# Normalizing the rests of q and k in place, loading raw weights one step further ahead, and two new orders in a fused attention and SwiGLU kernel

**Chip, cores, metric.** One core of one Trainium2 chip. The metric is the device time of one execution in microseconds (us); the kernel before takes 1638.8 us (median of 4 runs). TensorE is written PE, VectorE DVE, ScalarE ACT, GpSimd POOL and the DMA-issuing SyncE SP, as in the profiles.

## The reference, cut to what matters

```python
# q, k, v: (8, 12, 448, 64); d_model 768, d_ff 1536; the FFN weights come as float64
q_n = q / sqrt(mean(q*q, -1) + 1e-6) * g_q          # k_n likewise with g_k
attn = softmax(q_n @ k_n.T / 8)                     # per batch entry and head
x    = (attn @ v) as (3584, 768)
xn   = x / sqrt(mean(x*x, -1) + 1e-6) * rms_g
g    = xn @ w_gate
out  = (g * sigmoid(g) * (xn @ w_val)) @ w_out
```

## The kernel before

A sequence of 448 rows is three tiles of 128 rows and a *rest* of 64. Heads are worked on in pairs: a *group* `g` is one pair of one sequence, six groups make a sequence. While PE does the attention of sequence b+1, the products of the FFN of sequence b fill its gaps. Four parts matter here.

**The rests.** Rests of q lie on 64 partitions, rests of k on the other 64. q's are normalized in place; k's stay as they are, and their factor `rr` is applied later, as a scale of the exponential:

```python
def norm_rests(b, lo, hi):
    ...                                        # ACT squares, DVE sums them into ms
    def rms():                                 # POOL
        rq = small.tile([D, n, 2], F32, name="rq")
        nc.gpsimd.tensor_scalar(ms, ms, D * 1e-6, None, ALU.add)
        nc.gpsimd.tensor_tensor(rq, ms[0:D], mhalf[0:D, ...], ALU.pow)
        nc.gpsimd.tensor_tensor(rest[0:D], rest[0:D], rq..., ALU.mult)
    def rms_k():                               # POOL, two more pows
        for place in range(2):
            nc.gpsimd.tensor_tensor(st["rr", b][own(place), lo:hi], ms[own(1), :, place], mhalf[own(1), 0:n], ALU.pow)
...
nc.scalar.activation(e, ps[:, 0:S], ACT.Exp, scale=st["rr", b][:, hp:hp + 1])   # ACT, rests' exponential
```

**The conversion of the weights.** 72 pieces of float64 are turned into float32 on the chip, in a pipeline of turns that are strewn between the other work:

```python
raw_pool, cv_pool = pool("c_raw", 6), pool("c_cv", 6)
def convert():                                 # turn n
    ...
    if 0 <= n - 4 < len(pieces): ...           # POOL adds the halves of piece n-4 (frees raw and cv)
    if 0 <= n - 3 < len(pieces): ...           # DVE joins piece n-3
    if 0 <= n - 2 < len(pieces): ...           # ACT splits piece n-2 (needs raw, takes a cv buffer)
    if n < len(pieces): ...                    # SP loads piece n into a raw buffer
    if 0 <= n - 6 < len(pieces): keep(...)     # SP stores the finished piece
    if turn_of["n"] == TURNS:                  # conversion over: cv buffers become weight blocks
        free_w.extend(cv_pool.tile([128, BW], F32, name="top") for _ in range(6))
```

Together with 25 fixed ones this gives 31 weight blocks of 128x384 from then on.

**Derived weights.** The FFN of later sequences uses seven products instead of eight (Strassen). The sums of weights that this needs, T1 to T4, are made once, by DVE, while sequence 1's FFN runs. Each needs a free block, so the number of blocks decides how early a derivation can stand in the program (which is built, in a fixed order, by counting free blocks). Seven such products make a *quad*; sequence 1 begins with its first.

**The order on PE** in the first groups (0 to 6, which the prediction calls the *direct stage*), and just before sequence 0's FFN:

```python
# groups 1 to 6                          # group 7
pe(lambda: score(g, (1,)))               pe(lambda: values(g - 1))
pe(lambda: sums(g - 1))                  pe(lambda: score(g, (1,)))
pe(lambda: score(g, (2,)))               pe(lambda: rms_x(0))
                                         pe(lambda: score(g, (2,)))
                                         pe(lambda: sums(g - 1))
                                         pe(lambda: norm_x(0))
```

Of the kernel before, what the change touches and what calls it, by code (L numbers as in the profile page):

```python
# [8 lines left out]
F32 = mybir.dt.float32  # L9
I32 = mybir.dt.int32  # L10
U32 = mybir.dt.uint32
I64 = mybir.dt.int64
ALU = mybir.AluOpType
ACT = mybir.ActivationFunctionType
# [8 lines left out]
NPAIR = H // 2  # L23
# [312 lines left out]
def safe_scores(  # L336
# [22 lines left out]
    def pool(name, bufs, **kw):  # L359
        return ctx.enter_context(tc.tile_pool(name=name, bufs=bufs, **kw))  # L360
# [3 lines left out]
    qk_pool, v_pool, qn_pool, qkT_pool = pool("c_qk", 4), pool("c_v", 3), pool("c_qn", 1), pool("c_qkT", 2)  # L364
    e_pool, tmp, y_pool, rest_pool = pool("c_e", 11), pool("c_tmp", 1), pool("c_y", 2), pool("c_rest", 2)
    x_pool, s_pool, slots = pool("c_x", 4), pool("c_xs", 3), pool("c_slots", 1)
    raw_pool, cv_pool = pool("c_raw", 6), pool("c_cv", 6)
    scratch = pool("c_dram", 1, space=DRAM)
    ps_s, ps_m, ps_f = pool("c_ps_s", 4, space=PSUM), pool("c_ps_m", 1, space=PSUM), pool("c_ps_f", 3, space=PSUM)

# [8 lines left out]
    def after(n, fn):  # L379
        due.append((now["t"] + n, fn))  # L380
# [14 lines left out]
    def own(j):  # L395
        return slice(j * D, (j + 1) * D)
# [42 lines left out]
    def norm_rests(b, lo, hi):  # L439

        if b >= B:
            return
        n = hi - lo
        rest = st["rest", b][:, lo:hi]
        sq = tmp.tile([128, n, 2, D], F32, name="sq", tag="sq", bufs=2)
        nc.scalar.activation(sq, rest, ACT.Square)
        if lo == 0:
            st["rr", b] = tmp.tile([128, NPAIR], F32, name="rr", tag="rr", bufs=2)
        ms = small.tile([128, n, 2], F32, name="msr")
        after(1, lambda: nc.vector.tensor_reduce(out=ms, in_=sq, axis=AX_X, op=ALU.add))  # L450

        def rms():
            rq = small.tile([D, n, 2], F32, name="rq")
            nc.gpsimd.tensor_scalar(ms, ms, D * 1e-6, None, ALU.add)
            nc.gpsimd.tensor_tensor(rq, ms[0:D], mhalf[0:D, 0:2 * n].rearrange("p (n h) -> p n h", h=2), ALU.pow)
            nc.gpsimd.tensor_tensor(rest[0:D], rest[0:D], rq.unsqueeze(3).to_broadcast([D, n, 2, D]), ALU.mult)

        def rms_k():
            for place in range(2):
                nc.gpsimd.tensor_tensor(st["rr", b][own(place), lo:hi], ms[own(1), :, place], mhalf[own(1), 0:n], ALU.pow)  # L460

        after(1 if b == 0 else 2, rms)
        after(2, rms_k)

    def direct(g):

# [93 lines left out]
    def rests(g):  # L560

        if g < NG:
            ps = ps_s.tile([128, 512], F32, name="sc", tag="s")
            for r in (own(0), own(1)):
                nc.tensor.matmul(ps[r, 0:S], lhsT=st["kT", g][r, LAST], rhs=st["qT", g][r, :], start=True, stop=True)  # L565
        if g:
            b, hp = divmod(g - 1, NPAIR)
            vr, e = st["vr", b][:, hp], st["e", g - 1, "rest"]
            av = st["av", g - 1] = ps_m.tile([128, 512], F32, name="av", tag="m")
            for j in range(2):  # L570
                nc.tensor.matmul(av[own(j), 0:S], lhsT=vr[across(j)], rhs=e[across(j)], start=True, stop=False,
                                 skip_group_check=True)
            if direct(g - 1):
                den = st["den", g - 1] = ps_f.tile([128, 512], F32, name="den", tag="f")
                for j in range(2):
                    nc.tensor.matmul(den[own(j), 0:S], lhsT=ones[across(j)], rhs=e[across(j)], start=True, stop=False,
                                     skip_group_check=True)
        if g < NG:
            b, hp = divmod(g, NPAIR)
            e = st["e", g, "rest"] = e_pool.tile([128, S], F32, name="e")  # L580
            nc.scalar.activation(e, ps[:, 0:S], ACT.Exp, scale=st["rr", b][:, hp:hp + 1])  # L581

    def values(g):

# [115 lines left out]
    def block():  # L700

        if free_w:
            return free_w.pop(0), free_w
        return free_h.pop(0), free_h
# [8 lines left out]
    def data(key):  # L713
        return st[key][0][:, 0:BW]
# [34 lines left out]
            cols = moe_w_out[fc * 128:(fc + 1) * 128, n * HALF:(n + 1) * HALF]  # L749
            pieces.append((("wo", 0, *block_of(n, fc)), cols.rearrange("p (a n) -> p a n", a=1)))  # L750
    turn_of = {"n": 0}
    TURNS = len(pieces) + 6

    def home(key):
        if key[0] == "w":
# [3 lines left out]
    def keep(key):  # L759
        nc.sync.dma_start(out=home(key), in_=data(key))  # L760

    def convert():

        n = turn_of["n"]
        if n >= TURNS or not room(1):
            return False
        turn_of["n"] += 1
        if 0 <= n - 4 < len(pieces):
            key = pieces[n - 4][0]
            st[key] = block()  # L770
            lo, top = st.pop(("cv", n - 4))
            nc.gpsimd.tensor_tensor(data(key).bitcast(I32), top, lo, ALU.add)  # L772
        if 0 <= n - 3 < len(pieces):
            st["cv", n - 3] = join(*st.pop(("cv", n - 3)))
        if 0 <= n - 2 < len(pieces):
            st["cv", n - 2] = split(st.pop(("raw", n - 2)))
        if n < len(pieces):
            st["raw", n] = load_raw(pieces[n][1])
        if 0 <= n - 6 < len(pieces):
            keep(pieces[n - 6][0])  # L780
        if turn_of["n"] == TURNS:

            free_w.extend(cv_pool.tile([128, BW], F32, name="top") for _ in range(6))
        return True


# [345 lines left out]
    def gate_value_items(b):  # L1132

        if b == 0:
            return [(3 * S, 4 * (fc + 1) + 6, 0, fn) for fc in range(NFC) for fn in plain(fc)]
        return [(6 * HT, TURNS, 8 * (fp + 1) if b == 1 else 0, fn) for fp in range(NFP) for fn in quad(b, fp)]

    def out_items(b):
        if b >= FIRST_O:
            return [(NFP // 2 * HALF, TURNS, 0, fn) for fn in out_strassen(b)]  # L1140
        tiles = 3 + b % 2
        return [(NFC // OUT_PARTS * HALF, 4 * NFC + NFC * (n + 1) + 6, 0, lambda a=(b, n, i, part, i == tiles - 1): project_out(*a))
                for n in range(2) for i in range(tiles) for part in range(OUT_PARTS)]


# [108 lines left out]
    for g in range(NG + 1):  # L1254
        b, hp = divmod(g, NPAIR)
        if g:
            load_pair(g + 3)
        if hp == 2:
            for i in range(2):
                load_rests(b + 1, i, nc.sync)  # L1260
            load_v_rests(b + 1)
        if g == 0:
            pe(lambda: score(0, (0,)))
            pe(lambda: rests(0))
            pe(lambda: score(0, (1, 2)))
            squares(2, 0)
            squares(2, 1)
            for i in range(2):
                pe(lambda: turn(1, i))
            for _ in range(3):  # L1270
                convert()
            load_pair(3)
            load_v(2)
            convert()
            load_rows()
            continue
        if g <= NPAIR:
            pe(lambda: score(g, (0,)))
            squares(g + 2, 0)
            squares(g + 2, 1)  # L1280
            convert()
            if g > 1:
                pe(lambda: turn(g + 1, 0))
                some_rests(g)
                pe(lambda: turn(g + 1, 1))
            pe(lambda: rests(g))
            pe(lambda: values(g - 1))
            if g == 1:
                pe(lambda: turn(g + 1, 0))
                some_rests(g)  # L1290
                pe(lambda: turn(g + 1, 1))
            load_v(g + 2)
            convert()
            pe(lambda: score(g, (1,)))
            pe(lambda: sums(g - 1))
            pe(lambda: score(g, (2,)))
            convert()
            if g == 2:
                bound()
            continue  # L1300

        pe(lambda: (rests(g), score(g, (0,)) if g < NG else None))
        pe(lambda: values(g - 1))
        load_v(g + 2)
        if g == NPAIR + 1:
            pe(lambda: score(g, (1,)))
            pe(lambda: rms_x(0))
            pe(lambda: score(g, (2,)))
        pe(lambda: sums(g - 1))
        if g == NPAIR + 1:  # L1310
            pe(lambda: norm_x(0))
            begin(0, 15)
        elif g < NG:
            pe(lambda: score(g, (1, 2)))
        if hp:
            fill()
            squares(g + 2, 0)
            squares(g + 2, 1)
            pe(lambda: turn(g + 1, 0))
            some_rests(g)  # L1320
            fill()
            pe(lambda: turn(g + 1, 1))
            fill()
            continue
        fill(3)
        pe(lambda: turn(g + 1, 0))
        fill(1)
        pe(lambda: rms_x(b - 1))
        squares(g + 2, 0)
        squares(g + 2, 1)  # L1330
        pe(lambda: turn(g + 1, 1))
        fill(len(todo))
        begin(b - 1, 16)
        pe(lambda: norm_x(b - 1))
        fill()
# [41 lines left out]
```

## Time and profile before

| | before |
|---|---|
| time, median of 4 runs (range) | 1638.8 us (1636.4 to 1639.8) |
| PE busy, of a span of 1636.6 us | 1593.6 us |
| POOL / DVE / ACT busy | 678.3 / 857.5 / 475.7 us |
| mean granted clock of PE | 0.990 |

PE is the bound, so the reading is of its idle stretches. A row of an engine's timeline has the start (us), the time that the row covers (us), the engine, the source line, output and inputs, shapes, how many instructions, and in brackets the idle time before it and what ended that. Rows of PE in the first 300 us are shown with the prediction below. Here is how sequence 1's FFN begins (340.23), waits, and ends where its output projection begins (475.50); PE's timeline of the kernel before:

```profile
340.23 2.44 PE L887 MATMUL ff<-x,w 128*128 128x224 f32 x12
...
370.21 3.67 PE L887 MATMUL ff<-x,w 128*128 128x224 f32 x18 [2.02 <-ACT p L920]
...
399.99 1.40 PE L887 MATMUL ff<-xs,top 128*128 128x224 f32 x6 [1.39 <-DVE u L899]
...
467.43 0.55 PE L519 MATMUL tr<-ident,qk 128*128 128x128 f32 x3 [0.31 <-DVE kT L523]
...
475.50 4.69 PE L1085 MATMUL ff<-w,h 128*128 128x384 f32 x14
```

This stretch of 135.27 us, called *stretch 1* below, has 5.66 us of idle PE: the three waits shown and 0.81, 0.23 and 0.90 us on DVE's u.

And POOL's rows for the rests, from its groups of instructions (busy us and mean ns of one stand after the bar; with its smaller forms, rr comes to 34 instructions and 29.8 us):

```profile
L460 POOL TENSOR_TENSOR rr<-msr,mhalf 64x3 f32<-64x3 f32 x30 | 27.3, 911 | 1.8
L455 POOL TENSOR_TENSOR rq<-msr,mhalf 64x6 f32<-64x6 f32 x15 | 21.5, 1436 | 1.3
L456 POOL TENSOR_TENSOR rest<-rest,rq 64x384 f32<-64x384 f32 x15 | 13.6, 908 | 1.2
```

### The profile page before, as it was taken

To read this page: it belongs to the slowest core of one execution; us is meant where nothing else is said; L and a number is where in the kernel's file an instruction comes from. 1 tells how busy PE (TensorE), PEld (TensorE's weight loads), DVE (VectorE), ACT (ScalarE), POOL (GpSimd) and SP (SyncE) were. 2 spreads that over 40 slices of the span, in tenths; PEclk is the share of its full clock that TensorE was granted. 3 is DMA by queue.
4 is the path that set the end of the run, shared out by engine and by line. 5 is a ranking of instruction groups with operands and counts; after the bars stand their busy time and mean duration, and the time that the engine had idled before them with its cause. 6 is when DMAs were issued, how large, how long until landed. Compare 5 with 4: busy or idle time off the path is not lost.

```text
span 1636.6 us, 21588 instructions
## 1 busy us (share of the span) xinstructions
PE 1593.6 (97%) x7328; PEld 1124.5 (69%) x7328; DVE 857.5 (52%) x1490; ACT 475.7 (29%) x944; POOL 678.3 (41%) x706
## 2 busy tenths in 40 slices
PE   7979999998999999999999999999999999999998
PEld 3334445577865787758885588847877587969974
DVE  4879769569872354525564245533655235433431
ACT  5745454322232223222322223222232123100110
POOL 7857777445434442434542245324634322200000
PEclk8999999999999999999999999999999999999999
DMA  7656656557775654485554655556544564557651
GB/s 180 193 158 185 217 163 185 161 178 239 227 227 144 208 160 131 125 257 154 157 151 139 173 162 155 144 185 203 160 135 116 165 178 116 149 182 237 174 143 51
DMA packets 264587, 276.81 MB, mean 169 GB/s; under 512 B 79124, under 2 KB 261396, under 8 KB 264468
## 3 DMA queue, kind: packets, MB, share of 16 engines
q1 hardware_dynamic: 263540, 275.15, 56.4%
q8 instruction: 60, 0.98, 0.3%
q14 instruction: 59, 0.48, 0.1%
q10 hardware_dynamic: 800, 0.20, 0.1%
q0 software_dynamic: 128, 0.00, 0.0%
HBM read 235.93 MB, written 39.32 MB: 168 GB/s over the span
## 4 chain that ended last, share of the span: by engine, by line
PE 85%; DVE 6%; POOL 3%; DMA 2%; issue 1%; SPq 1%; ACT 1%; POOLq 0%; DVEq 0%; ACTq 0%
PE ff L887 38%; PE ff L1085 21%; PE sc L535 6%; PE av L588 6%; PE ff L982 3%; PE ff L1116 3%; PE den L601 2%; PE sc L565 2%; PE tr L519 2%; DVE rd L609 1%; POOL w L772 1%; DVE rd L605 1%; DVE w L844 1%; POOL rs L498 1%; POOL es L552 1%
## 5 line engine op out<-in xcount | busy, mean ns | idle before, releaser
L887 PE MATMUL ff<-x,w 128*128 128x224 f32 x1608 | 326.7, 353 | 3.7 <-ACT p L920 2.0
L887 PEld LDWEIGHTS ff<-x,w 128*128 128x128 f32 x1608 | 301.6, 190 | 12.7 <-issue 5.9
L545 POOL TENSOR_TENSOR es<-e 128x448 f32<-128x448 f32 x82 | 91.3, 1134 | 512.1 <-ACT e L539 512.1
L887 PE MATMUL ff<-xs,w 128*128 128x224 f32 x1248 | 256.3, 353 | 0.3 <-DVE cc L899 0.2
L887 PEld LDWEIGHTS ff<-xs,w 128*128 128x128 f32 x1248 | 234.0, 190 | 5.6 <-issue 4.6
L552 POOL TENSOR_TENSOR es<-es,e 64x448 f32<-64x448 f32 (+1 forms) x164 | 193.2, 1189 | 6.3
L609 DVE RECIPROCAL rd<-rd 128x448 f32<-128x448 f32 x41 | 121.0, 2952 | 142.0 <-ACT rd L608 142.0
L1085 PE MATMUL ff<-w,h 128*128 128x384 f32 x568 | 192.6, 487 | 0.0
L539 ACT ACTIVATE e<-sc,rs 128x448 f32<-128x448 f32 x288 | 162.8, 634 | 52.9 <-PE sc L535 51.3
L1085 PEld LDWEIGHTS ff<-w,h 128*128 128x128 f32 x568 | 106.4, 190 | 74.1 <-issue 3.9
L535 PE MATMUL sc<-qT,kT 64*128 64x448 f32 x576 | 141.2, 589 | 10.1 <-ACT e L581 7.5
L588 PE MATMUL av<-e,vt 128*64 128x448 f32 x576 | 119.4, 550 | 0.0
L535 PEld LDWEIGHTS sc<-qT,kT 64*128 64x128 f32 x576 | 55.5, 190 | 91.5 <-issue 73.7
L1116 PE MATMUL ff<-x,w 128*128 128x448 f32 x288 | 114.4, 551 | 3.3 <-DVE x L655 3.3
L498 POOL TENSOR_TENSOR rs<-ms,mhalf 128x12 f32<-128x12 f32 (+1 forms) x50 | 114.7, 2295 | 4.2
L1085 PE MATMUL ff<-w,so 128*128 128x384 f32 x302 | 104.6, 488 | 2.0 <-DVE y L1046 2.0
L899 DVE TENSOR_TENSOR cc<-ff,u 128x448 f32<-128x448 f32 x84 | 52.3, 623 | 87.3 <-PE ff L887 87.1
L1116 PEld LDWEIGHTS ff<-x,w 128*128 128x128 f32 x288 | 54.5, 194 | 56.2 <-issue 50.6
L772 POOL TENSOR_TENSOR w<-top,raw 128x384 int32<-128x384 int32 x72 | 76.9, 1083 | 35.7 <-DVE top L736 19.6
L588 PEld LDWEIGHTS av<-e,vt 128*64 128x64 f32 x576 | 37.2, 137 | 77.3 <-issue 73.9
L1085 PEld LDWEIGHTS ff<-w,so 128*128 128x128 f32 x302 | 56.5, 190 | 42.3 <-DVE y L1046 3.9
L887 PE MATMUL ff<-x,top 128*128 128x224 f32 x408 | 85.4, 354 | 0.0
(124 smaller groups left out, 1997.0 us busy)
## 6 DMA issues: line engine op xcount, KB each, us to landing
w<-kept SPq DMA_DIRECT2D x443, 192.0 KB, 3.1
w<-kept_o SPq DMA_DIRECT2D x270, 192.0 KB, 2.6
top<-kept SPq DMA_DIRECT2D x109, 192.0 KB, 3.2
kept<-w SPq DMA_DIRECT2D x90, 192.0 KB, 3.8
top<-kept_o SPq DMA_DIRECT2D x66, 192.0 KB, 2.8
qk<-in_q_dram SPq DMA_DIRECT2D x48, 192.0 KB, 3.5
qk<-in_k_dram SPq DMA_DIRECT2D x96, 96.0 KB, 3.3
vt<-in_v_dram SPq DMA_DIRECT2D x48, 192.0 KB, 2.5
```

The source lines that it names most:

```text
L498: nc.gpsimd.tensor_tensor(st["rs", g][:, cols], ms, mhalf[:, cols], ALU.pow)
L535: nc.tensor.matmul(ps[:, 0:S], lhsT=kT[r, c * 128:(c + 1) * 128], rhs=qT[r, :], start=True, stop=True)
L539: nc.scalar.activation(e, ps[:, 0:S], ACT.Exp, scale=rs[:, n:n + 1])
L545: nc.gpsimd.tensor_tensor(es, st["e", g, 0, j], st["e", g, 1, j], ALU.add)
L552: nc.gpsimd.tensor_tensor(es[r], es[r], e[r], ALU.add)
L588: nc.tensor.matmul(av[own(j), 0:S], lhsT=vt[:, j, c], rhs=st["e", g, c, j], start=False, stop=(c == NK - 1), skip_group_check=True)
L609: nc.vector.reciprocal(rd, rd)
L772: nc.gpsimd.tensor_tensor(data(key).bitcast(I32), top, lo, ALU.add)
L887: nc.tensor.matmul(bank[:, w * HT:(w + 1) * HT], lhsT=wt[:, c * 128:(c + 1) * 128], rhs=x[:, c, :], start=onto is None and w == c == 0, st ...
L899: nc.vector.tensor_tensor(add[name], ps[:, 0:S], add[other], ALU.add)
L1085: nc.tensor.matmul(ps, lhsT=a, rhs=data(("wo", b, name, c)), start=first and c == 0, stop=c == NFP - 1, skip_group_check=True)
L1116: nc.tensor.matmul(bank[w][:, 0:S], lhsT=data(key)[:, c * 128:(c + 1) * 128], rhs=st["x", 0, half][:, c, :], start=half == c == 0, stop=ha ...
```

## The change

Its intent: (a) normalize k's rests in place together with q's, which makes the two `rr` pows and the scale needless; (b) split a piece three turns after its load instead of two, so that ACT no longer stands in front of a load that has not landed; seven raw and four cv buffers take the same memory as six and six; (c) in the first groups, put the sums ahead of the later scores; (d) put the first normalization of x ahead of the last values and scores. The diff, cut to its core:

```diff
-    raw_pool, cv_pool = pool("c_raw", 6), pool("c_cv", 6)
+    raw_pool, cv_pool = pool("c_raw", 7), pool("c_cv", 4)                                     # b
...
-            nc.gpsimd.tensor_tensor(rq, ms[0:D], mhalf[0:D, 0:2 * n].rearrange(...), ALU.pow)
-            nc.gpsimd.tensor_tensor(rest[0:D], rest[0:D], rq.unsqueeze(3)..., ALU.mult)
-        def rms_k(): ...
+            nc.gpsimd.tensor_tensor(ms, ms, mhalf[:, 0:2 * n].rearrange(...), ALU.pow)        # a
+            nc.gpsimd.tensor_tensor(rest, rest, ms.unsqueeze(3)..., ALU.mult)
...
-            nc.scalar.activation(e, ps[:, 0:S], ACT.Exp, scale=st["rr", b][:, hp:hp + 1])
+            nc.scalar.activation(e, ps[:, 0:S], ACT.Exp)
...
-    add n-4, join n-3, split n-2, load n, keep n-6; TURNS = len(pieces) + 6                   (in words)
+    add n-5, join n-4, split n-3, load n, keep n-7; TURNS = len(pieces) + 7                   # b
-            free_w.extend(cv_pool.tile([128, BW], F32, name="top") for _ in range(6))
+            free_w.extend(cv_pool.tile([128, BW], F32, name="top") for _ in range(4))
...
-            pe(lambda: score(g, (1,)))
             pe(lambda: sums(g - 1))
-            pe(lambda: score(g, (2,)))
+            pe(lambda: score(g, (1, 2)))                                                      # c
...
+        if g == NPAIR + 1:
+            pe(lambda: rms_x(0))                                                              # d
         pe(lambda: values(g - 1))
...
-            pe(lambda: rms_x(0))
+            pe(lambda: norm_x(0))
             pe(lambda: score(g, (2,)))
         pe(lambda: sums(g - 1))
         if g == NPAIR + 1:
-            pe(lambda: norm_x(0))
```

Four cv buffers leave 29 weight blocks at the end, not 31. Two lists of FFN products, not shown here, count the extra turn too.

More of the change, by code (lines that the diff above doesn't have):

```diff
@@ L446, in norm_rests, with scale @@
         nc.scalar.activation(sq, rest, ACT.Square)
-        if lo == 0:
-            st["rr", b] = tmp.tile([128, NPAIR], F32, name="rr", tag="rr", bufs=2)
         ms = small.tile([128, n, 2], F32, name="msr")
         after(1, lambda: nc.vector.tensor_reduce(out=ms, in_=sq, axis=AX_X, op=ALU.add))
-        def rms():
-            rq = small.tile([D, n, 2], F32, name="rq")
+        def scale():
             nc.gpsimd.tensor_scalar(ms, ms, D * 1e-6, None, ALU.add)
-            nc.gpsimd.tensor_tensor(rq, ms[0:D], mhalf[0:D, 0:2 * n].rearrange("p (n h) -> p n h", h=2), ALU.pow)
-            nc.gpsimd.tensor_tensor(rest[0:D], rest[0:D], rq.unsqueeze(3).to_broadcast([D, n, 2, D]), ALU.mult)
-        def rms_k():
-            for place in range(2):
-                nc.gpsimd.tensor_tensor(st["rr", b][own(place), lo:hi], ms[own(1), :, place], mhalf[own(1), 0:n], ALU.pow)
-        after(1 if b == 0 else 2, rms)
-        after(2, rms_k)
+            nc.gpsimd.tensor_tensor(ms, ms, mhalf[:, 0:2 * n].rearrange("p (n h) -> p n h", h=2), ALU.pow)
+            nc.gpsimd.tensor_tensor(rest, rest, ms.unsqueeze(3).to_broadcast([128, n, 2, D]), ALU.mult)
+        after(1 if b == 0 else 2, scale)
     def direct(g):
@@ L578, in rests @@
         if g < NG:
-            b, hp = divmod(g, NPAIR)
             e = st["e", g, "rest"] = e_pool.tile([128, S], F32, name="e")
-            nc.scalar.activation(e, ps[:, 0:S], ACT.Exp, scale=st["rr", b][:, hp:hp + 1])
+            nc.scalar.activation(e, ps[:, 0:S], ACT.Exp)
     def values(g):
@@ L751, in safe_scores @@
     turn_of = {"n": 0}
-    TURNS = len(pieces) + 6
+    TURNS = len(pieces) + 7
     def home(key):
@@ L767, in convert @@
         turn_of["n"] += 1
+        if 0 <= n - 5 < len(pieces):
+            key = pieces[n - 5][0]
+            st[key] = block()
+            lo, top = st.pop(("cv", n - 5))
+            nc.gpsimd.tensor_tensor(data(key).bitcast(I32), top, lo, ALU.add)
         if 0 <= n - 4 < len(pieces):
-            key = pieces[n - 4][0]
-            st[key] = block()
-            lo, top = st.pop(("cv", n - 4))
-            nc.gpsimd.tensor_tensor(data(key).bitcast(I32), top, lo, ALU.add)
+            st["cv", n - 4] = join(*st.pop(("cv", n - 4)))
         if 0 <= n - 3 < len(pieces):
-            st["cv", n - 3] = join(*st.pop(("cv", n - 3)))
-        if 0 <= n - 2 < len(pieces):
-            st["cv", n - 2] = split(st.pop(("raw", n - 2)))
+            st["cv", n - 3] = split(st.pop(("raw", n - 3)))
         if n < len(pieces):
             st["raw", n] = load_raw(pieces[n][1])
-        if 0 <= n - 6 < len(pieces):
-            keep(pieces[n - 6][0])
+        if 0 <= n - 7 < len(pieces):
+            keep(pieces[n - 7][0])
         if turn_of["n"] == TURNS:
-            free_w.extend(cv_pool.tile([128, BW], F32, name="top") for _ in range(6))
+            free_w.extend(cv_pool.tile([128, BW], F32, name="top") for _ in range(4))
         return True
@@ L1134, in gate_value_items @@
         if b == 0:
-            return [(3 * S, 4 * (fc + 1) + 6, 0, fn) for fc in range(NFC) for fn in plain(fc)]
+            return [(3 * S, 4 * (fc + 1) + 7, 0, fn) for fc in range(NFC) for fn in plain(fc)]
         return [(6 * HT, TURNS, 8 * (fp + 1) if b == 1 else 0, fn) for fp in range(NFP) for fn in quad(b, fp)]
@@ L1141, in out_items @@
         tiles = 3 + b % 2
-        return [(NFC // OUT_PARTS * HALF, 4 * NFC + NFC * (n + 1) + 6, 0, lambda a=(b, n, i, part, i == tiles - 1): project_out(*a))
+        return [(NFC // OUT_PARTS * HALF, 4 * NFC + NFC * (n + 1) + 7, 0, lambda a=(b, n, i, part, i == tiles - 1): project_out(*a))
                 for n in range(2) for i in range(tiles) for part in range(OUT_PARTS)]
```

## The prediction

> **What bounds the kernel now.** I read the page first. TensorE (PE) is busy for 1593.6 of 1636.6 us, so only its 43 us of idle time, and whatever a lowered clock costs after an idle stretch, can be won. The forty slices (41 us each) show where.
>
> ```profile
> PE   7979999998999999999999999999999999999998
> POOL 7857777445434442434542245324634322200000
> PEclk8999999999999999999999999999999999999999
> ```
>
> PE is short of work in the first 400 us and at the very end; from slice 6 on it nearly always reads 9 (90% or more). POOL, 41% on average, is at 7 and 8 tenths exactly in the first slices, and the granted clock dips there too. So the page's average says nothing of POOL; those stretches have to be read one by one. Then I read PE's timeline, where each idle stretch stands in brackets (start, us, instruction, idle before it and releaser).
>
> ```profile
> 84.76 0.55 PE L519 MATMUL tr<-ident,qn 128*128 128x128 f32 x3 [2.97 <-POOL qn L503]
> ...
> 97.01 1.76 PE L571 MATMUL av<-e,vr 64*64 64x448 f32 x4 [1.98 <-issue]
> ...
> 113.26 8.73 PE L1116 MATMUL ff<-x,w 128*128 128x448 f32 x18 [3.30 <-DVE x L655]
> ...
> 197.35 3.88 PE L535 MATMUL sc<-qT,kT 64*128 64x448 f32 x8 [4.07 <-ACT e L581]
> 201.16 5.57 PE L1116 MATMUL ff<-x,w 128*128 128x448 f32 x12
> ...
> 229.51 3.85 PE L535 MATMUL sc<-qT,kT 64*128 64x448 f32 x8 [3.46 <-ACT e L581]
> ```
>
> These stretches, with 1.31 at 71.68 (qn again), make most of the loss. The others: 6.1 us up to 7.6 us and 1.70, 0.72, 2.94, 1.82 until 22.5 us (start), 4.4 us at 370 to 406, 0.90 at 444.79, some 7 us after the last matmul. The last of those is untouched.
>
> Why is the exponential of the rests (e L581) late at 229? ACT's timeline, then POOL's, then the DMA queue's (SP):
>
> ```profile
> 218.98 0.56 ACT L728 ACTIVATE top<-raw 128x384 f32<-128x384 f32 x1 [2.67 <-DMA raw<-in_moe_w_out_dram]
> ...
> 227.96 0.55 ACT L728 ACTIVATE top<-raw 128x384 f32<-128x384 f32 x1 [7.97 <-DMA raw<-in_moe_w_out_dram]
> 228.41 0.53 ACT L729 ACTIVATE raw<-raw 128x384 int32<-128x384 uint32 x1
> 228.85 0.61 ACT L581 ACTIVATE e<-sc,rr 128x448 f32<-128x448 f32 x1
> ```
>
> ```profile
> 221.43 1.86 POOL L460 TENSOR_TENSOR rr<-msr,mhalf 64x3 f32<-64x3 f32 x2
> 223.37 5.85 POOL L772 TENSOR_TENSOR w<-top,raw 128x384 int32<-128x384 int32 x6
> ```
>
> ```profile
> 224.41 0.33 SPq L719 DMA_DIRECT2D raw<-in_moe_w_out_dram  x1
> ```
>
> The chain: POOL normalizes rests (msr, rq, rest, two rr) and is six conversion turns behind; the first add of the six ends at 224.4; it frees a raw buffer; the load is issued at 224.41 and lands at 227.96; ACT, which stood at the split of that piece, splits it (0.9 us) and only then runs e L581, which frees the score bank for which PE waits. The stall at 197 is the same with the load at 191.91.
>
> **What the Trainium skill says.** (1) "TensorE: Matmul & The Clock Gate", Part 1: after an idle window of about 3.4 us the array's clock is halved, until a busy window has passed. The trace agrees: 8 score passes take 3.88 and 3.85 us after the two long stalls against 1.77 in most places, and 18 of L1116 take 8.73 against 6.93. (2) "GPSIMD Engine Reference", 2.1 Instruction dispatch: each core works on its own 16 partitions, so 64 or 128 partitions should cost the same. The trace agrees: es adds over 64x448 take 1178 ns, over 128x448 1199; pow on 64x6 1.35 to 1.44 us, on 128x6 1.36. (3) "Perfetto Trace Analysis", Tensor Engine Instruction (MATMUL, LD_WEIGHTS): ACT, DVE and GPSIMD are strict FIFO. Agrees: ACT idled 7.97 us before a split with the ready e L581 behind it. (4) "DMA: Bandwidth & Descriptors", Anatomy of one DMA: the issuing sequencer waits for semaphores, not the DMA engine. Agrees: the queue's waits list L719 behind POOL's w with 92.4 us in 25 waits from 100 to 340 us.
>
> **The change, part by part.** The built order of instructions is the same on PE except in 44 places among its first 252 matmuls, so the rest of PE's work is equal.
>
> (a) Rests in place. Gone are 34 rr (29.8 us on POOL, group row L460); rq and the product now cover 128 partitions instead of 64, which (2) says is free. So each normalization is some 1.9 us shorter on POOL.
> - Start: the two rr of 1.15 us at 11.63 go, so the rest for the second transpose comes at 18.3 instead of 19.5: -1.2.
> - From 57 to 84 us POOL has no pause. It loses 2.16 (at 60.84) and 1.86 (at 74.41). qn is 2.2 earlier for the 1.31 stall and 4.0 earlier for the 2.97 stall: -4.3.
>
> (b) One step more ahead, seven raw and four cv buffers. The piece split at a turn was loaded a turn earlier, behind an add done before the burst. But a split now takes the cv buffer of the piece four before, so it waits for the add of two turns ago, the third of the six, without a DMA after it. At 229: burst ends 1.9 earlier at 221.5, three adds of 0.98 to 224.4, split 0.9, e from 225.3 to 225.9; PE asks at 226.0. At 197: burst ends at 188.5, three adds to 191.6, e from 192.5 to 193.1; PE asks at 193.3. Both stalls go, just. -4.07 and -3.46, and the clock: (3.88-1.77)+(5.57-4.67)=3.0 and 2.1. Sum -12.6.
>
> (c) Sums before the later scores. DVE's reciprocal (2.97) and product (0.62) start 0.95 earlier. The three small av waits (0.20, 0.29, 0.36) go: -0.85. The 1.98 at 97.01 becomes about 1.1, too short to halve the clock (1.76+1.73+1.10 there against 0.97+0.95+1.02, 1.65): -2.5.
>
> (d) First norm before the values. Its chain (msx, DVE, pow 1.02, rb, six scalings of 0.6) then lies beside values 2.4, score 0.95, score 0.95 and sums 2.4 on PE. Scaling starts some 3.4 us before the first ff; ff waits for one scaling each, not for all. The 3.30 goes and its clock penalty 8.73-6.93=1.8: -5.1.
>
> Debits. The direct stage is nearly full on DVE (19.0 of 20 us at 60 to 80): +0.7. Edges of (b): +0.3. Sequence 1 (340 to 475 us) gets its weights derived later: conversion ends one turn later, and 29 weight blocks are left over instead of 31. In the built order DVE has 4 derivations fewer done at the first quad, and in quads 2 and 5 derives T3 and T4 (T2 too, just before) only after the reciprocal and the eight so sums. From the DVE rows there (0.5 to 1.5 us each): one more before an already late copy at 370 (+1.0), two more before u at 399 less four after it (+0.6), some three more before kT at 467 (+1.9): +3.5.
>
> Sum: 1.2+4.3+12.6+0.85+2.5+5.1=26.6 won, 4.5 lost, 22.1 net: 1638.8-22.1, so **1616.5 us**.
>
> **Rivals.**
> - The new wait takes the old one's place: with four cv buffers the third add comes later than I worked out (the six adds take up to 1.03 each, the margin is 0.1 to 0.2 us). For it: the thin margins. Against it: a DMA of 3.6 to 3.9 us is no longer in the chain. If half of each stall and the clock penalties stay: about +8, 1625.
> - DVE becomes the bound, in the direct stage and in sequence 1, where PE already waits for u and p. For it: late derivations in the built order, and a stall of 3 us would bring the slow clock. Then +6 to +9: 1623 to 1626.
> - Loads: two weight blocks fewer starve the main stage. Against it: after 340 us no wait of PE is put down to a DMA. It would cost everywhere: 1640. I give it 2%.
> - Cleaner than thought: derivations fit into idle DVE time, the start gains more clock: 1609 to 1611.
>
> **Range and chances.** 26.6 of the 43+12 us of idle and clock loss is what the change can reach; faster by over 2% needs 1606, that is 33 us, beyond all terms. Both large rivals together end near 1630. Range 1608 to 1627; faster 0.04, within 2% 0.95, slower 0.01.
>
> **What would show it.** Right: no PE stall above 1.5 us between 60 and 300 us except about 1 at L571, 8 score passes always near 1.8 us; rr gone, the 64-partition groups of msr and rest now at 128 with about the same ns; ACT's splits waiting for POOL w instead of DMA. New stalls before quads 2 and 5 of sequence 1. Wrong: ACT's rests still late by 2 us or more (rival 1), more than 10 us of idle PE between 340 and 475 us (rival 2), or an ff stall on DMA.

## The result, and the profile after

The changed kernel takes 1620.6 us (median of 4 runs, 1619.0 to 1621.2) against 1638.8 us. Ratios are the mean time of one kernel's fast runs over that of the other's of the same rounds, so not quite the ratio of these medians: 0.989, 95% interval 0.987 to 0.991. That is 1.1% faster, within the 2% of "same", inside the range, and 4.1 us above the point predicted.

| | before | after |
|---|---|---|
| PE busy / span, us | 1593.6 / 1636.6 | 1587.8 / 1619.2 |
| POOL busy, us | 678.3 | 649.3 |
| mean granted clock | 0.990 | 0.995 |
| first product of the FFN at, us | 113.26 | 103.24 |
| first quad of sequence 1 at, us | 340.23 | 316.54 |
| stretch 1, us (idle in it) | 135.27 (5.66) | 141.60 (8.60) |
| first output projection of sequence 1 at, us | 475.50 | 458.14 |
| from there to the end of the span, us | 1161.1 | 1161.1 |

These are times of the profiled executions. The last row says that what follows stretch 1 takes as long as before. Up to the first quad 23.7 us are won, and stretch 1 gives 6.3 back: 17.4 us, the whole difference of the spans.

The page's slices after (each 40 us):

```profile
PE   7999999999999999999999999999999999999998
POOL 6867877444523344324632444334443322100000
PEclk9999999999999999999999999999999999999999
```

PE's third and tenth slices, 7 and 8 before, now read 9, and so does the first slice of the clock, 8 before. PE's timeline after, at the places that were shown of before with the prediction:

```profile
79.67 0.55 PE L511 MATMUL tr<-ident,qn 128*128 128x128 f32 x3 [1.36 <-POOL qn L495]
...
91.97 0.97 PE L563 MATMUL av<-e,vr 64*64 64x448 f32 x4 [1.88 <-issue]
...
103.24 7.03 PE L1107 MATMUL ff<-x,w 128*128 128x448 f32 x18
...
181.02 1.78 PE L527 MATMUL sc<-qT,kT 64*128 64x448 f32 x8
...
207.24 2.49 PE L527 MATMUL sc<-qT,kT 64*128 64x448 f32 x8 [0.42 <-ACT e L572]
```

The two stalls on the rests' exponential (4.07 and 3.46 us) are 0 and 0.42; the first FFN product waits for nothing, and 18 of them take 7.03 instead of 8.73 us; the stall on qn is halved, not gone; the wait at 92 us has nearly its old length, but the passes after it run at full speed (0.97 us for four instead of 1.76). The 8 passes at 207.24 still take 2.49 us and not the 1.78 of those at 181.02; the granted clock there was 1.00 (206.0 to 209.7 us), so this is not the slow clock.

ACT's timeline after, at the second of the two (POOL's run of adds began at 202.62 us):

```profile
203.66 0.57 ACT L719 ACTIVATE top<-raw 128x384 f32<-128x384 f32 x1 [5.37 <-POOL w L763]
...
205.74 0.57 ACT L719 ACTIVATE top<-raw 128x384 f32<-128x384 f32 x1
...
206.67 0.52 ACT L572 ACTIVATE e<-sc 128x448 f32<-128x448 f32 x1
```

The first split now waits for POOL's add (the cv buffer), not for a DMA, as (b) means it to; the exponential (e) follows the third split, at 206.67. POOL's rows for the rests after:

```profile
L452 POOL TENSOR_TENSOR msr<-msr,mhalf 128x6 f32<-128x6 f32 x15 | 21.2, 1414 | 1.2
L453 POOL TENSOR_TENSOR rest<-rest,msr 128x384 f32<-128x384 f32 x15 | 13.2, 883 | 1.2
```

Twice the partitions take no longer (1414 and 883 ns against 1436 and 908), and rr's 29.8 us are gone: POOL is busy for 29.0 us less.

And stretch 1 after, on PE's timeline:

```profile
316.54 2.44 PE L878 MATMUL ff<-x,w 128*128 128x224 f32 x12
...
347.51 6.34 PE L878 MATMUL ff<-x,w 128*128 128x224 f32 x24 [3.02 <-ACT p L911]
...
379.77 2.54 PE L878 MATMUL ff<-xs,w 128*128 128x224 f32 x12 [1.04 <-DVE u L890]
...
423.60 1.40 PE L878 MATMUL ff<-x,top 128*128 128x224 f32 x6 [1.49 <-DVE u L890]
...
448.38 0.55 PE L511 MATMUL tr<-ident,qk 128*128 128x128 f32 x3 [1.98 <-DVE kT L515]
```

Idle time is 8.60 us (those four, 0.75 and 0.32 on derived weights). Beyond that, 24 products after the first stall take 6.34 us where 24 elsewhere in stretch 1 take 4.70, and the 24 after the last one take 6.79 where such take 5.03: 3.4 us of slow clock (granted 0.76 from 347.5 to 354.0, 0.75 from 448.3 to 455.2). 2.94 more idle and 3.4 of clock are the 6.3 us given back. The clock part is not tied to the stalls: in the profiled executions of three other kernels below (only_b, no_a, before29), stalls of the same length at the same places were followed by a granted clock of 1.00, and stretch 1 took 138.4 us. DVE's timeline ahead of the last of these stalls:

```profile
441.16 1.22 DVE L956 TENSOR_TENSOR so<-h,so 128x128 f32<-128x128 f32 x1
442.30 0.55 DVE L835 TENSOR_TENSOR top<-w,w 128x384 f32<-128x384 f32 x1
442.77 3.36 DVE L835 TENSOR_TENSOR w<-w,w 128x384 f32<-128x384 f32 x3
...
448.11 0.22 DVE L515 COPY kT<-tr 128x64 f32<-128x64 f32 x1
```

After the sums for the projection (L953 to L956) come four derivations (L835), for which no block was free earlier; with those of the output weights (L855) they hold the copy of kT back until 448.3.

### The profile page after: what moved, and what is told of

Same layout as the page of the kernel before. It is cut to its first block, busy times and chain, and to the rows that moved or that the text cites. A ratio compares the mean times of both kernels' runs of the same rounds, so it can differ in the third digit from the quotient of the medians.

```text
span 1619.2 us, 21550 instructions
## 1 busy us (share of the span) xinstructions
PE 1587.8 (98%) x7328; PEld 1124.6 (69%) x7328; DVE 864.3 (53%) x1490; ACT 471.7 (29%) x944; POOL 649.3 (40%) x672
## 4 chain that ended last, share of the span: by engine, by line
PE 80%; DVE 6%; issue 0%; ACT 0%; POOL 0%; DVEq 0%; ACTq 0%
PE ff L878 39%; PE ff L1076 21%; PE av L579 5%; PE sc L527 5%; PE ff L973 3%; PE sc L557 2%; PE den L592 2%; PE tr L511 1%; DVE rd L600 1%; DVE w L835 1%; DVE top L726 1%; DVE top L727 1%; PE ff L1107 0%; DVE w L855 0%; DVE top L725 0%
## 5 line engine op out<-in xcount | busy, mean ns | idle before, releaser
L878 PE MATMUL ff<-x,w 128*128 128x224 f32 x1704 | 350.6, 355 | 3.0 <-ACT p L911 3.0
L878 PEld LDWEIGHTS ff<-x,w 128*128 128x128 f32 x1704 | 321.3, 191 | 14.6 <-issue 5.9
L878 PE MATMUL ff<-xs,w 128*128 128x224 f32 x1320 | 272.0, 354 | 1.0 <-DVE u L890 1.0
L878 PEld LDWEIGHTS ff<-xs,w 128*128 128x128 f32 x1320 | 248.7, 191 | 5.4 <-issue 3.9
L1076 PE MATMUL ff<-w,h 128*128 128x384 f32 x582 | 200.2, 487 | 0.0
L1076 PE MATMUL ff<-w,so 128*128 128x384 f32 x350 | 120.4, 488 | 2.0 <-DVE y L1037 2.0
L1076 PEld LDWEIGHTS ff<-w,so 128*128 128x128 f32 x350 | 65.5, 190 | 48.4 <-DVE y L1037 3.9
L1107 PEld LDWEIGHTS ff<-x,w 128*128 128x128 f32 x288 | 53.3, 190 | 50.8 <-issue 49.0
L613 POOL TENSOR_TENSOR ss<-ss,rd 128x448 f32<-128x448 f32 x40 | 47.4, 1185 | 76.9 <-ACT rd L612 76.9
```

Of the source, the lines that this page charges most:

```text
L878: nc.tensor.matmul(bank[:, w * HT:(w + 1) * HT], lhsT=wt[:, c * 128:(c + 1) * 128], rhs=x[:, c, :], start=onto is None and w == c == 0, st ...
L1076: nc.tensor.matmul(ps, lhsT=a, rhs=data(("wo", b, name, c)), start=first and c == 0, stop=c == NFP - 1, skip_group_check=True)
L1107: nc.tensor.matmul(bank[w][:, 0:S], lhsT=data(key)[:, c * 128:(c + 1) * 128], rhs=st["x", 0, half][:, c, :], start=half == c == 0, stop=ha ...
```

## The experiments

Each was timed in five rounds against the kernel before, on the same chip as the others of its set; all results were correct. The table gathers what the traces show; "score stalls" are the two stalls on the rests' exponential; the last column is the ratio to the kernel before, with its 95% interval. The times of the kernel before were 1640.35, 1640.04 and 1638.21 us (medians of 11 runs) in the three sets.

| kernel | blocks | first FFN product | score stalls | first quad | stretch 1 (idle) | median us | ratio |
|---|---|---|---|---|---|---|---|
| before | 31 | 113.26 | 4.07, 3.46 | 340.23 | 135.27 (5.66) | 1638.8 | 1 |
| after | 29 | 103.24 | 0, 0.42 | 316.54 | 141.60 (8.60) | 1620.6 | 0.9890 (0.9872-0.9907) |
| blocks31 | 31 | 102.94 | 0, 0.41 | 316.27 | 136.96 (5.64) | 1615.8 | 0.9854 (0.9839-0.9868) |
| no_b | 31 | 102.14 | 1.40, 2.19 | 322.04 | 136.97 (5.66) | 1622.9 | 0.9901 (0.9886-0.9915) |
| only_b | 29 | 113.45 | 1.22, 2.31 | 333.69 | 138.37 (8.59) | 1640.2 | 1.0002 (0.9986-1.0019) |
| only_a | 31 | 111.61 | 1.61, 1.33 | 332.56 | 135.28 (5.64) | 1630.0 | 0.9936 (0.9923-0.9949) |
| only_c | 31 | 110.73 | 4.22, 3.44 | 337.90 | 135.27 (5.64) | 1637.3 | 0.9982 (0.9969-0.9995) |
| only_d | 31 | 109.93 | 4.24, 3.37 | 336.74 | 136.96 (5.65) | 1637.1 | 0.9977 (0.9964-0.9990) |
| no_a | 29 | 108.01 | 1.23, 2.31 | 325.16 | 138.37 (8.59) | 1627.7 | 0.9931 (0.9916-0.9947) |
| derive_pool | 31 | 102.24 | 0, 0.41 | 315.53 | 135.14 (6.03) | 1615.7 | 0.9856 (0.9842-0.9871) |
| before29 | 29 | 113.10 | 4.04, 3.50 | 340.08 | 138.38 (8.59) | 1644.4 | 1.0041 (1.0021-1.0061) |
| b_31 | 31 | 113.33 | 1.24, 2.34 | 333.64 | 135.27 (5.64) | 1632.6 | 0.9965 (0.9953-0.9978) |
| sq3 | 31 | 102.06 | 0, 0.42 | 315.38 | 134.70 (4.81) | 1613.4 | 0.9849 (0.9835-0.9863) |

My theory after the first comparison was A: the two missing blocks put the derivations later in the program, and that is the debit of stretch 1. The rival B: PE comes to stretch 1 some 24 us earlier and meets a DVE that is no further. The rival C: the conversion ends a turn later.

### blocks31: the changed kernel with 31 blocks again

```diff
             free_w.extend(cv_pool.tile([128, BW], F32, name="top") for _ in range(4))
+            ring = [raw_pool.tile([128, 2 * BW], F32, name="so", tag="raw") for _ in range(7)]
+            last = ring.pop()
+            free_w.extend(last[:, i * BW:(i + 1) * BW] for i in range(2))
+            st["ring"] = ring            # the six others serve in turn, as the raw pool did
```

> The changed kernel with one edit: when the conversion ends, the seventh raw buffer is cut into two weight blocks, so 31 blocks are left over as in the kernel before (the changed kernel has 29). In the built program the derivations then stand among the products exactly where the kernel before has them; the pipeline of the conversion stays that of the changed kernel. Measure: the stretch from the first matmul of sequence 1's first quad to the first matmul of its output projection, 135.3 us before (5.7 of it idle) and 141.6 us after (8.6 idle, the rest slow clock). Theory A (the two missing blocks make the derivations late): the stretch returns to 135 to 136.5 us, the stall of 3.0 us on p shrinks to 2 or less without slow clock, and the whole takes 1614 to 1616 us. Theory B (TensorE reaches sequence 1 some 24 us earlier and finds VectorE no further, whatever the blocks): the stretch stays at 140 us or more, 1619 to 1621 us. Theory C (the conversion's end one turn later): as B.

Measured: 1615.8 us, idle time in stretch 1 5.64 us, the same six waits as before, to 0.02 us. PE's timeline of this version:

```profile
346.24 6.49 PE L882 MATMUL ff<-x,w 128*128 128x224 f32 x24 [2.00 <-ACT p L915]
...
445.16 0.55 PE L511 MATMUL tr<-ident,qk 128*128 128x128 f32 x3 [0.31 <-DVE kT L515]
```

Theory A holds; B and C fall, since PE arrives as early here (316.27) and the conversion ends as late as in the changed kernel. One thing differs from what was expected: the stall of 2.00 us was followed by a slow clock (6.49 us instead of 4.70, granted clock 0.74), hence 136.96 us and not 135.3. Its ratio lies below that of the changed kernel (interval up to 0.9868 against from 0.9872), so this version beats both, as far as ratios from two sets can be compared.

### no_b and only_b: without part (b), and part (b) alone

```diff
 no_b:   the changed kernel, with convert(), the two pools, TURNS and free_w as before
 only_b: the kernel before, with those lines as after
```

> The changed kernel with part (b) undone: six raw and six cv buffers and the old conversion pipeline; rests in place and both new orders stay. Theory A (blocks): the stretch of sequence 1 is 135 to 136.5 us as before, since the 31 blocks are back. Theory B (earlier arrival): it is 139 us or more. On the two stalls at the score passes after the fill (4.07 and 3.46 us before, 0 and 0.42 after): if the buffers of (b) were what removed them, they stay at 2.2 and 1.6 us (the burst on VectorE's neighbour POOL is 1.9 us shorter, the load of 3.6 us stays in the chain), the splits wait for a DMA again; if the shorter normalization alone was enough, both are under 0.5 us. Time: A with stalls kept 1618 to 1621 us; B with stalls kept 1624 to 1628; A without stalls 1614.

> The kernel before with part (b) alone: seven raw and four cv buffers, load one step more ahead. Everything up to 190 us as before (first ff at 113 us). Theory A (blocks): the two stalls shrink from 4.07 and 3.46 to some 2 us each (the normalization is still 1.9 us longer), the slow clock after them goes, first quad 8 to 9 us earlier at 331 to 332 us, and the stretch of sequence 1 grows from 135.3 to 141 us: 1635 to 1637 us in all, most of the gain eaten. Theory B (earlier arrival): TensorE arrives only 8 to 9 us earlier, not 24, so the stretch grows by a third of 6.3 us only, to 137 us: 1631 to 1633 us.

Stretch 1 has 5.66 us of idle PE in no_b, whose PE arrives at 322 us, and 8.59 us in only_b, whose PE arrives at 334 us: the blocks decide, not the arrival. The score stalls of no_b were expected at 2.2 and 1.6 us and came at 1.40 and 2.19; ACT there again waits for a load, as its timeline shows:

```profile
209.66 0.55 ACT L719 ACTIVATE top<-raw 128x384 f32<-128x384 f32 x1 [6.03 <-DMA raw<-in_moe_w_out_dram]
...
210.56 0.52 ACT L572 ACTIVATE e<-sc 128x448 f32<-128x448 f32 x1
```

In time, only_b was a miss: 1635 to 1637 us expected, 1640.2 measured. Its runs spread from 1634.7 us (mean clock 0.994) to 1642.1 (0.989), and the profiled one is among the fastest. In it the second score stall of 2.31 us kept the slow clock (8 passes in 3.88 us, granted clock 0.56), which I had expected to go. What the slower runs lost was not seen in a trace. Either way, part (b) alone wins nothing, although its first quad comes 6.5 us earlier. no_b took 1622.9 us where 1618 to 1621 were expected, and its stretch 1 of 136.97 us lies above the expected 136.5 (18 products after the stall on p took 5.36 us, at a granted clock of 0.68). The interval of its ratio overlaps that of the whole change, so the two cannot be told apart.

### only_a and no_a: part (a) alone, and the change without it

```diff
 only_a: the kernel before, with scale() for rms() and rms_k(), no rr, Exp without scale
 no_a:   the changed kernel, with rms(), rms_k(), rr and Exp(scale=rr) as before
```

> The kernel before with part (a) alone: rests of q and k normalized in place, no rr. The start wins 1.2 to 2.0 us, the two stalls on qn at 71 and 85 us lose 1.3 and 1.6 to 3.0 us, and at 197 and 229 us the load goes out 1.9 us earlier, so the stalls of 4.07 and 3.46 us become about 2.2 and 1.6 us; whether the slow clock after them (3.0 and 2.1 us) goes is not certain: 1624 us with it gone, 1629 with it kept. Theory A: stretch of sequence 1 unchanged at 135 us. Theory B: half of the debit, 138 us, and 3 us more in all. If (b) had been needless, both score stalls would be under 0.5 us here.

> The changed kernel with part (a) undone: q normalized in place, k through the scale rr; (b), (c) and (d) stay. Compared with the changed kernel: the start is 2 us later, the qn stalls stand between 1 and 3 us, first product of the gate at 107 to 109 us (103.2 with (a)). Score stalls after the fill: 1.2 and 2.3 us as in the run of (b) alone (0 and 0.42 with (a)): neither part alone removes them, both together do. Stretch of sequence 1 with 8.6 us idle, as it has 29 blocks. In all 1630 to 1634 us against 1620.6. Rival: if the shorter normalization mattered only at the start, the score stalls are under 0.5 us here and the whole takes 1625 us.

Part (a) alone wins 0.6%, and is the largest of the four. Its 1630.0 us are a little more than the 1629 expected for the worse case. The start won more than expected (PE was 3.2 us earlier at the first small wait on x), but the stalls on qn only went from 1.31 and 2.97 to 0.20 and 1.77 us, and the second was followed by a slow clock (0.62 from 81.08 to 85.60) that the kernel before does not have there: the first FFN product came 1.65 us earlier, where the expectation's terms make 4.1 or more. The score stalls in only_a were expected at 2.2 and 1.6 us and came at 1.61 and 1.33. Put beside only_b and no_a (1.2 and 2.3) and the changed kernel (0 and 0.42): neither (a) nor (b) alone removes these stalls, both together do. no_a was better than expected, 1627.7 us instead of 1630 to 1634; its stalls were as expected to 0.1 us, and after the second, 2.31 us, the clock stayed higher than in only_b (1.00 instead of 0.56; 2.48 us for 8 passes instead of 3.88).

### only_c and only_d: one order alone

```diff
 only_c: the kernel before, with sums(g - 1) ahead of score(g, (1, 2)) in groups 1 to 6
 only_d: the kernel before, with rms_x(0) ahead of values and norm_x(0) ahead of score(g, (2,)) in group 7
```

> The kernel before with part (c) alone: in the first six groups the sums stand ahead of the later scores. Theory D (gains of the parts add up, as the prediction's sum assumes): the three small waits (0.20, 0.29, 0.36 us) go, the wait of 1.98 us at the rests' products becomes about 1.1 with the clock full after it, so the first product of the gate starts 0.85 + 2.5 us earlier, near 110 us, and the whole loses 3 us against the kernel before (ratio 0.998). Theory E (POOL and VectorE set the pace from 57 to 97 us, TensorE only waits longer for the same thing): what the small waits give is taken back at the two stalls on qn (1.31 and 2.97 us before), which grow by it, VectorE's backlog keeps the later wait at 1.9 us, and the first product of the gate starts within 1 us of 113.3 or, if the slow clock after the wait goes, at 111.6; ratio 0.999 to 1.0005.

> The kernel before with part (d) alone: the first normalization of sequence 0 ahead of its last values. Nothing changes up to 97 us; the stall of 3.30 us before the first product of the gate goes, and with it the 1.8 us of slow clock in its 18 products (8.73 to 7.0 us): first product at 110.0 us, first quad at 335.2 us if the two score stalls (4.07 and 3.46 us) keep their size, ratio 0.997 (5 us won). Rival: POOL or VectorE, still busy with conversions, finish no earlier, so those two stalls grow by what is won: ratio 0.999 or more.

Theory D had the size right (first product 2.5 us earlier, 0.998) but not the way: the three small waits went, the later wait stayed at 1.85 us as theory E had it, with a slow clock after it (0.55 from 94.44 to 97.40), and the gain came at qn. PE's timeline of only_c:

```profile
69.65 0.55 PE L519 MATMUL tr<-ident,qn 128*128 128x128 f32 x3 [1.78 <-POOL qn L503]
...
82.64 0.55 PE L519 MATMUL tr<-ident,qn 128*128 128x128 f32 x3 [0.82 <-POOL qn L503]
```

Together these two are 2.60 us, 4.28 before: with the sums earlier, qn itself comes 2.1 us earlier. only_d gives the first product at 109.93 us, where 110.0 was expected; its score stalls kept their size within 0.2 us. Its first quad came at 336.74 instead of 335.2 and its ratio at 0.9977 instead of 0.997; where that difference arose was not traced. In stretch 1 the slow clock followed the stall on p (0.68), with the idle time unchanged.

The parts add up. The ratios of only_a, only_b, only_c and only_d are 0.64, -0.02, 0.18 and 0.23% below 1: 1.03% in sum, and the whole change gives 1.10%. With b_31 (below) for only_b the sum is 1.40%, and blocks31 gives 1.46%. Each of these ratios is uncertain by some 0.15%, so the close agreement is in part chance.

### before29: two blocks fewer and nothing else

```diff
-            free_w.extend(cv_pool.tile([128, BW], F32, name="top") for _ in range(6))
+            free_w.extend(cv_pool.tile([128, BW], F32, name="top") for _ in range(4))
```

> The kernel before with one number changed: of the six cv buffers only four are given to the weight blocks at the end of the conversion, so 29 are left over instead of 31; the pipeline of the conversion and everything else is the old one. Theory A (the two blocks alone make the debit of sequence 1): idle time there 8.6 us as in the changed kernel (5.6 with 31), with stalls of 3.0 on p and 2.0 on kT, first quad as before at 340 us, the stretch 138.4 to 141.6 us by whether the slow clock follows, the whole 3 to 6 us slower (ratio 1.002 to 1.004). Theory C (the conversion's end one turn later makes it): idle time stays 5.6 us, the whole within 1 us of the kernel before.

Measured: 1644.4 us, 0.41% slower; idle time 8.59 us, with the stalls of the changed kernel. PE's timeline:

```profile
371.05 2.54 PE L887 MATMUL ff<-x,w 128*128 128x224 f32 x12 [3.01 <-ACT p L920]
...
470.39 0.55 PE L519 MATMUL tr<-ident,qk 128*128 128x128 f32 x3 [1.97 <-DVE kT L523]
```

This makes the stalls of stretch 1 in a kernel that has nothing else of the change. Of the 6 to 7 us, 2.93 are idle PE; the other half was not in the profiled execution (138.38 us, no slow clock). Its runs go from 1639.5 us (mean clock 0.993) to 1649.4 (0.986), so the clock after longer stalls is the likely rest, though no trace caught it.

### b_31: part (b) with 31 blocks

```diff
 the kernel before with part (b) and the ring of blocks31
```

> The kernel before with part (b), and the seventh raw buffer cut into two blocks at the end, so that 31 are left over. Part (b) alone gave nothing (ratio 1.0002), though its first quad came 6.5 us earlier. Theory A: with the blocks back the idle time of sequence 1 is 5.6 us, first quad at 333.7 us as in (b) alone, and the whole is 3 to 6.5 us faster than before (ratio 0.996 to 0.998). If something else of (b) ate its gain (the clock, or a loss after sequence 1), the ratio stays at 0.999 or above.

1632.6 us, ratio 0.9965 where part (b) alone gave 1.0002; idle time 5.64 us. So (b) is worth 0.35% by itself, and all of it is lost by the two blocks. The later split and the division into seven and four buffers, which (b) changes together, were not tried apart.

### derive_pool: the output weights derived on POOL

```diff
 # in derive_o, on top of blocks31
-        nc.vector.tensor_tensor(data(key), a, b, ALU.subtract)
+        nc.gpsimd.tensor_tensor(data(key), a, b, ALU.subtract)
```

> The version with 31 blocks, with the 24 derivations of the output weights on POOL instead of VectorE (same tiles, same order among themselves). What is left of the idle time in sequence 1 (5.6 us: 2.0 on p, 1.4, 0.8, 0.2 and 0.9 on u, 0.3 on kT) stands behind VectorE's queue, which is busy for 107 of 137 us there against 60 on POOL. Theory F (the derivations of VectorE are what p and u wait for): 24 of some 0.7 us leave VectorE, the stall on p falls under 1 us, the idle time of sequence 1 to 2 or 3 us, and the whole to 1611 to 1613 us (1615.8 with 31 blocks alone). Theory G (VectorE's operations on two SBUF operands are themselves slowed by POOL's, 1.48 us instead of 0.55 while POOL adds): the added POOL work slows as many others, the idle time stays at 5 to 7 us, or new waits on es come, 1615 to 1619 us.

1615.7 us, the same as blocks31; idle time 6.03 us instead of 5.64. Three small waits went, but the one on u at 377 us grew from 1.39 to 3.06 us, and a later one from 0.90 to 1.22. Theory G holds. DVE's timeline of derive_pool before that stall:

```profile
367.58 1.22 DVE L962 TENSOR_TENSOR h<-h 128x128 f32<-128x128 f32 x1
...
373.02 0.28 DVE L963 TENSOR_TENSOR so<-h,so 128x128 f32<-128x128 f32 x1
373.22 1.48 DVE L839 TENSOR_TENSOR w<-w,w 128x384 f32<-128x384 f32 x1
```

The same kind of operation takes 0.28 us when POOL is quiet and 1.22 while POOL adds; a derivation takes 0.55 or 1.48 us. The Trainium skill says so ("SBUF — State Buffer", SBUF: two separate sides): DVE with two inputs in SBUF and POOL reading SBUF exclude one another, for the whole instruction. The trace agrees: DVE's adds with one input in PSUM (u, cc) stay at 0.61 us throughout. So POOL, though busy for only 60.0 of 137 us there in blocks31, has little room to give to DVE. The totals of stretch 1 show it: with 20 of its 191 instructions there moved, DVE was busy for 106.6 us instead of 107.2, and POOL for 80.0.

### sq3: three buffers for squares

```diff
 # on top of blocks31
-    e_pool ... = pool("c_e", 11)
+    e_pool ... = pool("c_e", 10)
-        sq = tmp.tile(..., name="sq", tag="sq", bufs=2)      # in all three places
+        sq = tmp.tile(..., name="sq", tag="sq", bufs=3)
```

> The version with 31 blocks, with three buffers for the squares instead of two, paid for by one of the eleven e buffers. The stall of 2.0 us on p that sequence 1 has in both kernels: ACT's copy p stands behind the square of the rests, which waits for a square buffer that VectorE's sums of squares free, and those stand behind derivations. Theory H (the buffer is what p waits for): that stall goes, idle time of sequence 1 to 3.6 us, the slow clock of 1.7 us after it too, 1612 to 1614 us (1615.8 with 31 blocks alone). Theory I (the bank or VectorE itself is late by as much, or ten e buffers stop ACT elsewhere): 1615 us or more, with new waits of score passes on e.

The stall of 2.0 us on p went, as theory H has it, and the slow clock after it; but 1.15 us of it came back at once, since DVE is as late as before for u and cc. PE's timeline:

```profile
350.88 2.54 PE L882 MATMUL ff<-x,top 128*128 128x224 f32 x12 [0.40 <-DVE u L894]
```

Idle time 4.81 us (3.6 expected), 1613.4 us (1613.1 to 1614.1), no new waits on e. It is the lowest time; its interval overlaps that of blocks31, so that it is better is likely, not shown.

## Why the prediction was right, and where its sum was off

The time was in the range and the mechanism was the predicted one; the result is 4.1 us above the point. Term by term (us; the measured column is from the profiled executions):

| term | predicted | measured |
|---|---|---|
| start, up to the scores at 22.5 | +1.2 | +2.0 (22.47 to 20.43) |
| two stalls on qn | +4.3 | +2.7 (1.31 and 2.97 to 0.24 and 1.36) |
| three small waits on x | +0.85 | +0.85 |
| wait at the rests' products, with its clock | +2.5 | +1.75 (0.10 idle, 1.65 clock) |
| first norm, with its clock | +5.1 | +5.0 (3.30 and 8.73 - 7.03) |
| score stalls, with their clock | +12.6 | +12.0 (226.97 - 213.30 from first FFN product to first quad, less the 1.70 of the line above) |
| DVE full, edges, and what is left over | -1.0 | -0.6 |
| stretch 1 | -3.5 | -6.3 |
| sum | +22.1 | +17.4 |

- **Rests in place.** "64 or 128 partitions should cost the same" held (rows above), and so did the 29.8 us of rr. The step that failed is the one for qn: "qn is 2.2 earlier for the 1.31 stall and 4.0 earlier for the 2.97 stall". qn came 5.1 us earlier (84.76 to 79.67), more than predicted, but PE asked for it 3.5 us earlier too (81.79 to 78.31), since everything ahead of it had won. A stall shrinks by the difference of the two; the working moved one end only.
- **Load ahead.** "Both stalls go, just" held: 0 and 0.42. That it takes both parts was in the working (the burst 1.9 us shorter, then three adds instead of a load), and only_a, only_b, no_a and no_b show it. "8 score passes always near 1.8 us" did not hold after the 0.42: they took 2.49 us, as in no_a after both stalls (2.49 and 2.48), with a granted clock of 1.00 each time. So some 0.7 us of each 8 passes that the prediction put down to the clock was probably not the clock.
- **Sums ahead.** "Becomes about 1.1" failed: 1.88 us. The sums ended at 87.4, but DVE began the reciprocal only at 88.26, after joins of the conversion that stand before it; the product then ended at 91.9 and PE went on at 91.97. The reason for the wait had been DVE's start after the sums; it became DVE's own backlog. That the clock would stay up came true, but not for the reason given, a wait "too short to halve the clock": after a wait of 1.85 us in only_c, and of 2.00 us in no_a, the granted clock was 0.55 and 0.60, while it was 1.00 after waits of 1.80 to 1.89 us in all five kernels that have both (a) and (c). So 1.65 of the 1.75 us won here did not come from a shorter wait, and (c) alone did not bring it; why the clock stayed up is open.
- **First norm ahead.** As predicted.
- **Readings.** Two lines were read too simply. POOL's first slices are 7857777, so the third, where PE dips, is at 5 and not at 7 or 8 tenths, and PEclk reads below 9 in the first only. And the pow on 64x6, put at 1.35 to 1.44 us, took 1.63 and 1.67 in the two bursts that were worked out (185.69 and 218.46). Neither changes a term of the sum.
- **Stretch 1.** The place and cause were predicted: later derivations by 29 blocks, stalls at p (+1.0: measured 2.02 to 3.02), u, and kT (+1.9: measured 0.31 to 1.98). The idle part came out as 2.94 us where 3.5 stood. The mis-sized term is the clock: the sum had none for the debit, although the second rival named it ("a stall of 3 us would bring the slow clock"); it cost 3.4 us in the profiled execution, and nothing in those of only_b, no_a and before29, so its size in a single execution is chance. before29, b_31 and blocks31 show that the blocks alone make the stalls. The prediction gave a second cause beside the blocks, "conversion ends one turn later"; blocks31, which keeps that, shows that it plays no part.
- **Rivals.** The first, a new wait in the old one's place, left 0.42 us. The second came true in part, by its clock; its sign, more than 10 us of idle PE in stretch 1, did not appear (8.60). The third, starving loads, did not appear: no stall in stretch 1 is put down to a DMA.

## What to carry to other kernels

When a change shifts buffers between pools, follow the buffers to the end of their lives: here two weight blocks that were missing once the conversion was over cost about as much as the deeper pipeline gave by itself (0.41 and 0.35%), and cutting the spare raw buffer into two blocks brought it back. When several waits in a row shrink, move both ends of each, the producer's and the waiter's. Look after each stall whether the slow clock followed, and don't price that from one trace: here the same stall brought it in one execution and not in another. An engine with free time can take over little work if the two exclude one another: look at the duration of the same instruction with and without the other one running.

## What the Trainium skill lacked or had wrong

- "TensorE: Matmul & The Clock Gate", Part 1, ties the lowered clock to an idle window of about 3.4 us, and its closing rules to gaps over about 3 us. Here waits of 1.57 us (only_b, at 83.31: granted clock 0.54 over the next 3.1 us), 1.98 us (before, at 97.01: 0.50) and 2.00 us (blocks31, at 346.24: 0.74) were followed by it, and waits of 2.97 us (before, at 84.76) and 3.02 us (only_b, at 364.66: 24 products in 4.81 us) were not, with a clock of 1.00; the changed kernel's wait of 3.02 us (at 347.51: 6.34 us for 24 products, 0.76) was. The page does say that the window runs freely and that frequent short idle times can make the clock swing; a figure for how short a single wait can be was missing.
- "SBUF — State Buffer" states the exclusion of DVE and POOL, but gives no size for this pair of operations: 0.28 us became 1.22 (128x128) and 0.55 became 1.48 (128x384) next to POOL's float32 adds.
